# Retention, routing and expert in one kernel: one state copy, a first block cut by chunks, and rank comparisons on scores spread in PSUM

## The chip, the cores and the metric

The kernel runs on one core of one Trainium2 chip. The metric is the device time of one launch in microseconds (us). Names of engines: PE is TensorE (matrix products; PEld is its weight load), DVE is VectorE, ACT is ScalarE, POOL is GpSimd, SP is SyncE, which here only issues DMAs.

## The reference, cut to what matters

```python
# q, k, v: (batch 4, heads 8, tokens 768, 64)
gamma = 1 - 2 ** (-5 - arange(H))
for t in range(S):                                  # decayed state, one 64x64 matrix a head
    state = gamma * state + einsum('bhd,bhe->bhde', k[:, :, t], v[:, :, t])
    y[:, :, t] = scale * einsum('bhd,bhde->bhe', q[:, :, t], state)
x = y.transpose(0, 2, 1, 3).reshape(B, S, H * D)    # (4, 768, 512)
scores = einsum('bsd,d->bs', x, w_gate)
out = x.copy()
for b in range(B):                                  # 128 tokens of highest score a batch
    top = argpartition(-scores[b], 128)[:128]
    h = maximum(x[b, top] @ w1, 0)                  # 512 -> 1024
    out[b, top] = x[b, top] + sigmoid(scores[b, top])[:, None] * (h @ w2)
```

## The kernel before, in words

The recurrence is computed by chunks of 128 tokens. Twelve *blocks* of 256 tokens (i = 0 to 11, three a batch) hold two chunks each (c = 0, 1). For a block, q, k and v arrive as float32 tiles `qf`, `kf`, `vf` (512 KB each, in 2 KB packets; one partition holds eight tokens of one pair of heads). POOL scales q and v by the powers of gamma (`qc`, `vc`, line 387), ACT or POOL casts k (`kc`), all to bfloat16 "row" tiles. PE turns them (`tk`, `tq`, `tv`, line 404), ACT copies the turned tiles out of PSUM (`ek`, `eq`, `ev`, line 407), and for k and v PE turns them back into token order (`tkb`, `tvb`, line 418; copies `ekb`, `evb`, line 421).

For each chunk PE forms the scores of q against k in eight products on 64 rows of the array (`sc`, line 464, tile `ps`), DVE multiplies them with the causal mask (`mk`, line 468, tile `A`), and PE adds the part from the state and the part within the chunk (`y`, lines 475 and 478, tile `py`). The state of a batch accumulates in one PSUM tile `pst` of 4 x 128 columns: four 128x128 products a chunk (`up`, line 442) hold two heads each, and only the two 64x64 blocks on the diagonal are wanted. So two copies of 64 partitions a chunk (`es`, line 175, 64x256) move the wanted blocks to a bfloat16 tile `S`, whose other blocks POOL sets to zero at the start (`cz`, line 260). ACT copies `py` out (`ey`, tile `xo`), DVE multiplies it with the gate weights and sums (`ga`, line 501), and SP stores `xo` (`st`, line 506).

Routing needs the rank of each token's score within its batch of six chunks. For chunk J, PE spreads its 128 scores over all partitions (`pr`, line 523, a float32 transposition), ACT or DVE copies them to a float32 tile `row` (`cp`), and DVE compares: `cd` (line 530) the chunk with itself under a triangular mask `tri`, `co` (line 537) with the J earlier chunks out of `row`, one instruction of J x 128 elements. `cnt`, `rk`, `oh`, `ix`, `ic` make the list of chosen tokens. Then the expert: rows are gathered by an indirect DMA (`gat`; batch 3 picks them by a product instead), turned (`tn`), multiplied with w1 and w2 (`hu`, `dn`), scaled (`ad`) and scattered back (`sa`). The weights arrive in eight loads of 512 KB and are cast by ACT and POOL (`wc`).

The order of the work is a table, `ORDER`: each item is a task, `@A`, `@D` or `@P` name the engine where a task may run on several, and `+n` puts n filler products on PE ahead of it (line 243, operand `fill`). Each engine works through its own tasks in that order. `DEPTH` gives the number of buffers of each tile. PSUM tiles of scores, turned tiles and spread scores share one pool of five buffers, `px`.

The first block is loaded in halves by the parity of the head (two 256 KB transfers a tensor, 2 KB packets), and a tile is turned only once both halves are there.

Of the kernel before, what the change touches and what calls it, by code (L numbers as in the profile page):

```python
# [15 lines left out]

PICKED = (3,)
# [3 lines left out]
HALVES = (0,)  # L21

GATE_POOL = ()
DEPTH = {'qf': 5, 'kf': 5, 'vf': 5, 'qb': 4, 'kb': 4, 'vb': 4, 'qT': 3, 'kT': 3, 'A': 8, 'S': 6, 'xo': 15, 'junk': 2, 'sc': 3, 'row': 2, 'g': 2, 'racc': 3, 'oh': 2, 'idx': 4, 'xg': 3, 'xgT': 2, 'e': 4, 'gt': 4, 'hT': 2, 'xr': 2, 'yb': 6, 'px': 5, 'py': 2, 'pst': 1}

ORDER = """
cf lk.0.1 cd0 cp1 cd1 lv.0.1 lv.0.0 ca3 lk.0.0 kc.0.1@A cz lq.0.0 lw cp2 kc.0.0@A tk.0+13 lq.0.1 vc.0.1 lq.1.0 ca2
lk.1.0 lv.1.0 vc.0.0 lq.2.0 cp3 tv.0 cd3 lk.2.0 qc.0.0 lv.2.0 ek.0 lk.3.0 ev.0 ws wb@D tvb.0 lq.3.0 tkb.0 ekb.0 qc.0.1
qc.1.1 tq.0+2 evb.0 qc.1.0 up.0.0 eq.0 kc.1.1@A es.0.0.0@D vc.1.1 es.0.0.1@D vc.1.0 qc.2.1 sc.0.0+1 mk.0.0.0 sc.0.1
qc.2.0 kc.1.0@A vc.2.1 vc.2.0 up.0.1 tq.1 kc.3.0@P kc.3.1@P lv.3.0 lq.4.0 tk.1 lk.5.0 mk.0.0.1 y.0.0 lk.4.0 mk.0.1.0  # L30
eq.1 ek.1 tkb.1+1 ekb.1 mk.0.1.1 qc.3.0 ga.0.0 es.0.1.1@A sc.1.1 tv.1 mk.1.1.0 sc.1.0 mk.1.1.1 mk.1.0.0 kc.2.1@A y.0.1
tq.2+1 qc.3.1 ev.1 kc.2.0@A tk.2 eq.2 vc.3.0 vc.3.1 ek.2 mk.1.0.1 tvb.1 evb.1 sc.2.0+2 tv.2 es.0.1.0@D ey.0.1@D qc.4.1
lq.5.0 lv.5.0 ey.0.0@A sc.2.1 ga.0.1 up.1.0 mk.2.0.0 ev.2 qc.4.0 lv.4.0 mk.2.0.1 lq.6.0 y.1.0 mk.2.1.0 pr.0.0 lk.6.0
es.1.0.1@A tk.3 es.1.0.0@A tvb.2 y.1.1 ga.1.0 kc.4.0@P cp.0.0@D mk.2.1.1 tq.3 ek.3 evb.2 tkb.2 lq.7.0 ey.1.0@A lk.9.0
eq.3 cd.0.0 lk.7.0 ekb.2 pr.0.1 up.1.1 kc.4.1@P ga.1.1 cd.0.1 pr.0.2 sc.3.0+1 es.1.1.0@A qc.5.0 kc.5.1@P cp.0.1@A tv.3
co.0.1 es.1.1.1@A qc.5.1 ev.3 y.2.0+1 up.2.0 cp.0.2@D mk.3.0.0 mk.3.0.1 cd.0.2 sc.3.1 co.0.2 kc.5.0@A mk.3.1.0
# [93 lines left out]
def kernel(ctx: ExitStack, tc: tile.TileContext, q, k, v, w_gate, w1, w2, capacity, out):  # L130
# [52 lines left out]
    def load(i, nm):  # L183
        b, r = divmod(i, R)
        src = {"q": q, "k": k, "v": v}[nm]
        base = src[b, :, r * W:(r + 1) * W, :]
        parts = 2 if i in HALVES else 1
        tasks = []
        t = P.buf(nm + "f", [128, 1024], FT)
        for part in range(parts):  # L190
            n = 2 // parts
            ap = bass.AP(tensor=base.tensor, offset=base.offset + part * n * S * D,
                         ap=[[8 * D, W // 8], [2 * S * D, HP], [S * D, n], [1, 8 * D]])

            def issue(e, part=part, n=n, ap=ap):
                nc.sync.dma_start(t[:].rearrange("p (n x) -> p n x", n=2)[:, part * n:(part + 1) * n], ap)  # L196

            tasks.append(P.add(f"l{nm}.{i}.{part}", "SP", issue, bufs=[t]))
        loaded[nm, i] = (t, tasks)
# [13 lines left out]
    gv = consts.tile([128, R, 2, 8], FT, name="gv")  # L213
    lgm = consts.tile([128, 2], FT, name="lgm")
    causal = consts.tile([128, C], BF, name="causal")
    tri = consts.tile([128, C], BF, name="tri")
# [501 lines left out]
```

## Time and profile before

| | |
|---|---|
| Median of 3 runs | 106.24 us (106.13 to 106.3) |
| The profiled execution | 106.56 us, its span (first to last instruction) 104.7 us |
| Busy in the span | PE 91.5 us (87%), DVE 80.3 (77%), POOL 77.4 (74%), ACT 76.6 (73%) |
| DMA | 31.43 MB, 15091 packets, mean 300 GB/s |
| Mean granted TensorE clock | 0.978 |

A row of the timeline reads: start, duration, engine, source line, operation, tile written <- tiles read, number of merged instructions, and in brackets the idle time ahead of it with what ended it. A group of instructions reads: line, engine, operation, count | busy us, mean ns of one | idle us ahead of them, what ended it. The busy time of PE covers products that wait inside it, so the distance from the start of one group to the start of the next tells more than the duration.

### The profile page before, as it was taken

To read this page: it belongs to the slowest core of one execution; us is meant where nothing else is said; L and a number is where in the kernel's file an instruction comes from. 1 tells how busy PE (TensorE), PEld (TensorE's weight loads), DVE (VectorE), ACT (ScalarE), POOL (GpSimd) and SP (SyncE) were. 2 spreads that over 40 slices of the span, in tenths; PEclk is the share of its full clock that TensorE was granted. 3 is DMA by queue.
4 is the path that set the end of the run, shared out by engine and by line. 5 is a ranking of instruction groups with operands and counts; after the bars stand their busy time and mean duration, and the time that the engine had idled before them with its cause. 6 is when DMAs were issued, how large, how long until landed. Compare 5 with 4: busy or idle time off the path is not lost.

```text
span 104.7 us, 3641 instructions
## 1 busy us (share of the span) xinstructions
PE 91.5 (87%) x1416; PEld 71.6 (68%) x1416; DVE 80.3 (77%) x249; ACT 76.6 (73%) x179; POOL 77.4 (74%) x109
## 2 busy tenths in 40 slices
PE   4949879299999999899989999999899999999900
PEld 1326557168968888887878898789689985878500
DVE  5207397807999999998999999999999998254320
ACT  4444683674899999999899999999999976222200
POOL 7599669999998994979679936999893284370630
PEclk9999999967999999999999999999999999999997
DMA  1997999999999999981079999999957999972152
GB/s 22 303 299 277 336 404 390 386 386 386 391 382 386 388 387 384 388 313 41 0 271 283 343 356 401 408 418 410 386 161 228 321 399 400 388 273 108 12 88 100
DMA packets 15091, 31.43 MB, mean 300 GB/s; under 512 B 1249, under 2 KB 1249, under 8 KB 15074
## 3 DMA queue, kind: packets, MB, share of 16 engines
q1 hardware_dynamic: 14450, 29.37, 77.5%
q0 software_dynamic: 624, 1.84, 6.2%
q8 instruction: 11, 0.18, 0.7%
q14 instruction: 6, 0.05, 0.1%
HBM read 23.86 MB, written 7.34 MB: 298 GB/s over the span
## 4 chain that ended last, share of the span: by engine, by line
DMA 31%; ACT 22%; PE 14%; POOL 12%; SPq 9%; issue 8%; POOLq 1%; ACTq 0%
DMA out_dram<-xo 12%; DMA wf<-in_moe_w_dram 11%; DMA vf<-in_v_dram 8%; SPq L196 5%; ACT S L175 5%; POOL vr L387 5%; ACT xo L175 4%; SPq L506 3%; PE ps L464 2%; POOL w1s L179 2%; ACT vT L407 2%; ACT qT L407 2%; ACT kr L175 2%; ACT vb L421 2%; POOL qr L387 2%
## 5 line engine op out<-in xcount | busy, mean ns | idle before, releaser
L468 DVE TENSOR_TENSOR A<-ps,causal 128x512 bf16<-128x512 f32 x48 | 30.7, 683 | 4.1 <-PE ps L464 4.0
L387 POOL TENSOR_TENSOR qr<-qf,gq 128x512 bf16<-128x512 f32 x24 | 24.7, 1046 | 6.8 <-ACT kb L421 2.6
L387 POOL TENSOR_TENSOR vr<-vf,gv 128x512 bf16<-128x512 f32 x24 | 24.5, 1046 | 3.3 <-DMA vf<-in_v_dram 2.0
L501 DVE SCALAR_TENSOR_TENSOR junk<-py,wgB 128x512 bf16<-128x512 f32 x24 | 16.4, 683 | 0.5 <-PE py L478 0.4
L175 ACT ACTIVATE S<-pst 64x256 bf16<-64x256 f32 x37 | 14.0, 377 | 0.4
L537 DVE TENSOR_SCALAR_CACHE_REDUCE g<-row,sc,racc 128x128 bf16<-128x128 f32 (+4 forms) x20 | 13.1, 667 | 0.2
L175 ACT ACTIVATE xo<-py 128x512 f32<-128x512 f32 x22 | 13.0, 600 | 0.2
L404 PE MATMUL tk<-ident,kr 128*128 128x128 bf16 x96 | 7.5, 221 | 3.5 <-ACT kr L175 3.4
L464 PE MATMUL ps<-qT,kT 64*128 64x128 bf16 x192 | 10.0, 222 | 0.3 <-ACT kT L407 0.2
L175 ACT ACTIVATE kr<-kf 128x512 bf16<-128x512 f32 x10 | 6.2, 628 | 5.3 <-DMA kf<-in_k_dram 3.3
L478 PE MATMUL py<-vb,A 128*128 128x64 bf16 x192 | 9.5, 193 | 0.0
L404 PEld LDWEIGHTS <-kr 128*128 128x128 bf16 x96 | 5.8, 98 | 4.8 <-ACT kr L175 4.4
L421 ACT ACTIVATE kb<-tkb 128x512 f32<-128x512 f32 x12 | 7.2, 603 | 2.2 <-PE tkb L418 2.1
L464 PEld LDWEIGHTS <-kT 64*128 64x128 bf16 x192 | 5.8, 95 | 4.4 <-issue 1.0
L670 POOL DMA_INDIRECT out_dram<-xr,idx x4 | 4.7, 1168 | 5.4 <-DVE xr L664 3.0
L442 PE MATMUL pst<-vb,kb 128*128 128x128 bf16 x80 | 7.7, 219 | 1.0 <-ACT S L175 0.4
L179 POOL CAST kr<-kf 128x512 bf16<-128x512 f32 x14 | 8.3, 613 | 0.1
L530 DVE SCALAR_TENSOR_TENSOR g<-pr,sc,tri 128x128 bf16<-128x128 f32 x24 | 8.1, 345 | 0.3 <-ACT row L175 0.2
L407 ACT ACTIVATE vT<-tv 128x512 f32<-128x512 f32 x12 | 7.2, 599 | 1.4 <-PE tv L404 1.3
L475 PE MATMUL py<-S,qT 128*128 128x128 bf16 x80 | 7.7, 219 | 0.5 <-ACT xo L175 0.3
L655 PE MATMUL pd<-w2s,hT 128*128 128x512 bf16 x32 | 8.1, 379 | 0.0
L478 PEld LDWEIGHTS <-A 128*128 128x128 bf16 x192 | 7.9, 98 | 0.2
(112 smaller groups left out, 212.3 us busy)
## 6 DMA issues: line engine op xcount, KB each, us to landing
out_dram<-xo SPq DMA_DIRECT2D x24, 256.0 KB, 5.7
qf<-in_q_dram SPq DMA_DIRECT2D x11, 512.0 KB, 9.6
kf<-in_k_dram SPq DMA_DIRECT2D x11, 512.0 KB, 10.7
vf<-in_v_dram SPq DMA_DIRECT2D x11, 512.0 KB, 10.6
wf<-in_moe_w_dram SPq DMA_DIRECT2D x8, 512.0 KB, 7.7
kf<-in_k_dram SPq DMA_DIRECT2D x2, 256.0 KB, 3.9
vf<-in_v_dram SPq DMA_DIRECT2D x2, 256.0 KB, 3.5
qf<-in_q_dram SPq DMA_DIRECT2D x2, 256.0 KB, 3.9
```

Source lines behind the costliest of these rows:

```text
L175: nc.scalar.activation(dst, src, AF.Copy)
L179: nc.gpsimd.tensor_copy(dst, src)
L387: nc.gpsimd.tensor_mul(row[x][:, :, hf, :], half(x, hf), g[:, r, hf, :, None].to_broadcast([128, 8, D]))
L404: nc.tensor.transpose(t1[:, j].rearrange("p g h -> p (g h)"), row[x][:, j].rearrange("p e d -> p (e d)"), ident)
L407: return P.add(f"e{x}.{i}", "ACT", lambda e: nc.scalar.activation(words(T, "x t y").rearrange("p (x g j) -> p x g j", x=2, j=8), words(t1, ...
L421: return P.add(f"e{x}b.{i}", "ACT", lambda e: nc.scalar.activation(dst[:].rearrange("p j h d -> p (j h d)").bitcast(FT), t2[:].rearrange(" ...
L464: nc.tensor.matmul(ps[par][:, dd, :], kT[rr, dd // 2, ts, dd % 2], qT[rr, dd // 2, ts, dd % 2], start=True, stop=True, skip_group_check=True)
L468: mk = [P.add(f"mk.{i}.{c}.{par}", "DVE", lambda e, par=par: nc.vector.tensor_mul(A[par][:], ps[par][:], causal[:, None, :].to_broadcast([ ...
L478: nc.tensor.matmul(py[c][:, h, :], A[h % 2][:, h // 2, :], vb[:, c, h, :], start=(J == 0 and h == 0), stop=True, skip_group_check=True)
L501: bt["gate", J] = P.add(f"ga.{i}.{c}", "DVE", lambda e, c=c, J=J, junk=junk: nc.vector.scalar_tensor_tensor(junk[:], py[c][:].opt(), 1.0, ...
L530: nc.vector.scalar_tensor_tensor(bt["g"][:, lo + J, :], pr[:, :C], bt["sc"][:, J:J + 1], tri, OP.is_ge, OP.mult, accum_out=bt["racc"][:, J ...
L537: nc.vector.tensor_scalar(bt["g"][:, lo:lo + J, :].rearrange("p i t -> p (i t)"), bt["row"][:, :J * C], bt["sc"][:, J:J + 1], bt["racc"][: ...
```

## The change

Four edits, and a new table of order with new numbers of buffers.

**One copy a state.** Each head now has its own product: eight of 64x64 a chunk in place of four of 128x128, written to the 64 partitions of that head. At a batch's first chunk one product of zeros (128x512) clears the whole PSUM tile. `S` then takes one copy of 128x512. POOL no longer sets the `S` tiles to zero. For the last block of a batch only one of its two chunks of k is turned back.

**The first block by chunks.** Block 0 is loaded by chunks of 128 tokens (256 KB, 1 KB packets; four tokens of both heads of a pair lie in one partition), and each chunk is scaled, turned and copied by itself. That needs tables of powers of its own (`pos4`, `gq4`, `gv4`: one small instruction on POOL, two on DVE, four on ACT).

**Scores spread in PSUM.** For chunk J, PE spreads the scores of all chunks 0 to J again, up to four in one PSUM tile, and DVE compares straight from PSUM: one instruction up to J = 3, two for J = 4 and 5. The tile `row` and its copies are no longer used. The number of spreads rises from 24 to 84, that of comparing instructions falls from 44 to 32.

**Buffers and fillers.** Row tiles (`qb`) 4 to 6, `kT` 3 to 4, `vf` 5 to 4, `xo` 15 to 16; weights are loaded through the buffers of q and not of v. The fillers rise from 34 to 45, of which 28 are half as wide.

```diff
-HALVES = (0,)
+SPREAD = (0, 1, 2, 3)
+CHUNKED = (0,)
...
+        if i in CHUNKED:
+            for c in range(2):
+                ap = bass.AP(tensor=base.tensor, offset=base.offset + c * C * D,
+                             ap=[[4 * D, C // 4], [2 * S * D, HP], [S * D, 2], [1, 4 * D]])
+                tasks.append(P.add(f"l{nm}.{i}.{c}", "SP", lambda e, c=c, ap=ap: nc.sync.dma_start(
+                    t[:].rearrange("p (c n x) -> p c n x", c=2, n=2)[:, c], ap), bufs=[t]))
...
             def update(e, c=c, J=J):
-                for dd in range(HP):
-                    nc.tensor.matmul(pst[b][:, dd, :], kb[:, c, 2 * dd:2 * dd + 2, :].rearrange("p h d -> p (h d)"),
-                                     vb[:, c, 2 * dd:2 * dd + 2, :].rearrange("p h d -> p (h d)"), start=(J == 0 and dd == 0),
-                                     stop=True, skip_group_check=True)
+                if J == 0:
+                    nc.tensor.matmul(pst[b][:].rearrange("p h d -> p (h d)"), zero, fill, start=True, stop=True,
+                                     skip_group_check=True)
+                for h in range(H):
+                    hh = slice(64 * (h % 2), 64 * (h % 2) + 64)
+                    nc.tensor.matmul(pst[b][hh, h // 2, hh], kb[:, c, h, :], vb[:, c, h, :], start=False, stop=True,
+                                     skip_group_check=True)
...
-            st["es", b, J + 1] = [P.add(f"es.{i}.{c}.{par}", "ACT DVE", lambda e, Sb=Sb, hh=slice(64 * par, 64 * par + 64): copy(
-                e, Sb[hh, :, hh], pst[b][hh, :, hh]), after=[t_s, k_z], bufs=[pst[b], Sb]) for par in range(2)]
+            st["es", b, J + 1] = [P.add(f"es.{i}.{c}", "ACT DVE", lambda e, Sb=Sb: copy(e, Sb[:], pst[b][:]), after=[t_s],
+                                        bufs=[pst[b], Sb])]
...
+    def rank_spread(b, J):
...
+        for first in ((4, 0) if J > 3 else (0,)):
+            n = min(4, J + 1 - first)
+            pr = P.buf("px", [128, 512], FT, "pr")
+            def spread(e, first=first, n=n, pr=pr):
+                for I in range(n):
+                    nc.tensor.transpose(pr[:, I * C:I * C + C], bt["sc"][:, first + I:first + I + 1].to_broadcast([128, C]), identf)
...
+            def compare(e, first=first, n=n, pr=pr, near=near):
+                g = bt["g"][:, lo + first:lo + first + n, :].rearrange("p i t -> p (i t)")
+                if near:
+                    nc.vector.scalar_tensor_tensor(g, pr[:, :n * C], bt["sc"][:, J:J + 1], tri4[:, 4 * C - n * C:], OP.is_ge, OP.mult,
+                                                   accum_out=bt["racc"][:, J:J + 1])
+                else:
+                    nc.vector.tensor_scalar(g, pr[:, :n * C], bt["sc"][:, J:J + 1], bt["racc"][:, J:J + 1], OP.is_ge, OP.add,
+                                            accum_out=bt["racc"][:, J:J + 1])
```

Where the table moves instructions, at three places:

SP's queue at the start, before (tile names as above; the last figures are partitions x runs x elements):

```order
L196 DMA kf<-in_k_dram 128x1x512
L196 DMA vf<-in_v_dram 128x1x512 x2
L196 DMA kf<-in_k_dram 128x1x512
L196 DMA qf<-in_q_dram 128x1x512
L325 DMA wrow<-in_moe_w_gate_dram 1x512
L196 DMA qf<-in_q_dram 128x1x512
L196 DMA qf<-in_q_dram 128x2x512
```

The same place now (line 177 loads a chunk, line 181 a whole block):

```order
L177 DMA vf<-in_v_dram 128x2x256
L177 DMA qf<-in_q_dram 128x2x256
L177 DMA kf<-in_k_dram 128x2x256
L177 DMA qf<-in_q_dram 128x2x256
L177 DMA kf<-in_k_dram 128x2x256
L177 DMA vf<-in_v_dram 128x2x256
L181 DMA vf<-in_v_dram 128x2x512
```

The first three transfers now hold all of chunk 0, where they held all of v and one parity of k; behind block 0 stands v of block 1, where q of block 1 stood.

DVE among the tasks of blocks 1 to 3, before:

```order
L177 COPY row<-pr 128x128
L468 TENSOR_TENSOR A<-ps,causal 128x512 x2
L530 SCALAR_TENSOR_TENSOR g,racc<-pr,sc,tri 128x128
L537 TENSOR_SCALAR g,racc<-row,sc,racc 128x256
L468 TENSOR_TENSOR A<-ps,causal 128x512 x2
L501 SCALAR_TENSOR_TENSOR junk,sc<-py,wgB 128x512
L530 SCALAR_TENSOR_TENSOR g,racc<-pr,sc,tri 128x128
L537 TENSOR_SCALAR g,racc<-row,sc,racc 128x384
```

And now (line 506 is the mask, 538 the gate, 606 and 609 the comparisons out of PSUM):

```order
L506 TENSOR_TENSOR A<-ps,causal 128x512 x4
L538 SCALAR_TENSOR_TENSOR junk,sc<-py,wgB 128x512
L606 SCALAR_TENSOR_TENSOR g,racc<-pr,sc,tri_163 128x256
L506 TENSOR_TENSOR A<-ps,causal 128x512 x4
L161 COPY xo<-py 128x512
L606 SCALAR_TENSOR_TENSOR g,racc<-pr,sc,tri_163 128x384
```

The pair of comparisons has become one, and the copy to `row` is gone.

PE at a spread and an update of the state, before:

```order
L418 LDWEIGHTS kT
L418 MATMUL tkb<-ident,kT 128x128
L523 MATMUL pr<-identf,sc 128x128
L442 LDWEIGHTS kb
L442 MATMUL pst<-vb,kb 128x128
```

PE now, at the second spread of batch 0 and, in the same stretch, the last rows of an update:

```order
L515 LDWEIGHTS A
L515 MATMUL py<-vb,A 128x64
L596 MATMUL pr<-identf,sc 128x128 x2
L425 LDWEIGHTS vr
L425 MATMUL tv<-ident,vr 128x128
```

```order
L481 LDWEIGHTS kb
L481 MATMUL pst<-vb,kb 64x64
L512 LDWEIGHTS qT
L512 MATMUL py<-S,qT 128x128
L512 LDWEIGHTS qT
```

Chunk 1 now has two spreads in a row where one stood, and an update works on 64x64 pieces between groups that use the whole array.

More of the change, by code (lines that the diff above doesn't have):

```diff
@@ L32 @@
[L32 to L36, printed above, removed]
@@ L186, in load @@
         base = src[b, :, r * W:(r + 1) * W, :]
-        parts = 2 if i in HALVES else 1
         tasks = []
         t = P.buf(nm + "f", [128, 1024], FT)
[L190 to L198, printed above, removed]
+        if i in CHUNKED:
[5 more added lines that the diff above has]
+        else:
+            ap = bass.AP(tensor=base.tensor, offset=base.offset, ap=[[8 * D, W // 8], [2 * S * D, HP], [S * D, 2], [1, 8 * D]])
+            tasks.append(P.add(f"l{nm}.{i}.0", "SP", lambda e, ap=ap: nc.sync.dma_start(
+                t[:].rearrange("p (n x) -> p n x", n=2), ap), bufs=[t]))
         loaded[nm, i] = (t, tasks)
@@ L213 @@
     gv = consts.tile([128, R, 2, 8], FT, name="gv")
+    NK = len(CHUNKED)
+    assert list(CHUNKED) == list(range(NK)) and NK <= R
+    pos4_i = consts.tile([128, NK, 2, 4], I32, name="pos4_i")
+    pos4 = consts.tile([128, NK, 2, 4], FT, name="pos4")
+    gq4 = consts.tile([128, NK, 2, 2, 4], FT, name="gq4")
+    gv4 = consts.tile([128, NK, 2, 2, 4], FT, name="gv4")
     lgm = consts.tile([128, 2], FT, name="lgm")
     causal = consts.tile([128, C], BF, name="causal")
-    tri = consts.tile([128, C], BF, name="tri")
+    tri4 = consts.tile([128, (4 if SPREAD else 1) * C], BF, name="tri4")
+    tri = tri4[:, -C:]
     slot_i = consts.tile([128, C], I32, name="slot_i")
@@ L299, in c_act0, with c_act4, c_act5 @@
         nc.scalar.activation(pair, pair_i.bitcast(FT), AF.Copy)
+    def c_act4(e):
+        for par in range(2):
+            nc.scalar.activation(gq4[:, :, :, par, :], pos4, AF.Exp, bias=lnsc[:, 0:1], scale=lgp[:, par:par + 1])
+    def c_act5(e):
+        for par in range(2):
+            nc.scalar.activation(gv4[:, :, :, par, :], pos4, AF.Exp, scale=lgm[:, par:par + 1])
     def c_act2(e):
@@ L398, in turn @@
         def turn(x, cast, T):
-            t1 = P.buf("px", [128, 8, W // 8, HP], BF, "t" + x)
-            def go(e):
-                for j in range(8):
-                    nc.tensor.transpose(t1[:, j].rearrange("p g h -> p (g h)"), row[x][:, j].rearrange("p e d -> p (e d)"), ident)
-            t_1 = P.add(f"t{x}.{i}", "PE", go, after=cast + [k_p1], bufs=[row[x], t1, T], warm=warm(t1))
-            return P.add(f"e{x}.{i}", "ACT", lambda e: nc.scalar.activation(
-                words(T, "x t y").rearrange("p (x g j) -> p x g j", x=2, j=8),
-                words(t1, "j g h").rearrange("p (j g x) -> p x g j", j=8, x=2), AF.Copy), after=[t_1], bufs=[t1, T])
@@ new lines, in turn, with piece, go @@
+            if chunked:
+                return [piece(f"{i}.{c}", range(4 * c, 4 * c + 4), [cast[c]]) for c in range(2)]
+            return [piece(f"{i}", range(8), cast)] * 2
+        def back(x, e_1, T, dst):
+            def piece(name, cs, after):
+                t2 = P.buf("px", [128, len(cs), HP, 128], BF, "t" + x + "b")
+                def go(e):
+                    for k, c in enumerate(cs):
+                        for dd in range(HP):
+                            nc.tensor.transpose(t2[:, k, dd, :], T[:, dd // 2, C * c:C * c + C, dd % 2], ident)
+                t_2 = P.add(f"t{x}b.{name}", "PE", go, after=after, bufs=[T, t2, dst], warm=warm(t2))
+                return P.add(f"e{x}b.{name}", "ACT", lambda e: nc.scalar.activation(
+                    words(dst, "j h d")[:, 256 * cs[0]:256 * (cs[-1] + 1)], words(t2, "j h d"), AF.Copy), after=[t_2], bufs=[t2, dst])
+            cs = range(1 if x == "k" and r == R - 1 else 2)
+            if chunked:
+                done = [piece(f"{i}.{c}", [c], [e_1[c]]) for c in cs]
+            else:
+                done = [piece(f"{i}", cs, [e_1[0]])] * 2
+            return done
@@ L472, in y @@
             def y(e):
[L473 to L476 removed]
+                for dd in range(HP if J else 0):
+                    nc.tensor.matmul(py[c][:, 2 * dd:2 * dd + 2, :].rearrange("p h d -> p (h d)"), qT[:, dd // 2, ts, dd % 2],
+                                     S_of[b, J][:, dd, :], start=(dd == 0), stop=True, skip_group_check=True)
                 for h in range(H):
```

186 lines of the change are left out of this document (105 added, 81 removed).

## Prediction

> **What bounds the kernel now.** I read first the busy time by stretches of 12 us, because the shares of the whole span mix a start, a long middle and a tail. Columns: stretch, length, then busy us and count of PE, PEld, DVE, ACT and POOL, granted clock, DMA share, GB/s.
>
> ```profile
> 12.00:24.00 12.00, 9.12 (x127) 6.19 (x124) 7.95 (x16) 7.33 (x14) 10.68 (x12) 0.90 1.05 392
> 24.00:36.00 12.00, 11.87 (x206) 9.99 (x205) 11.44 (x33) 10.25 (x23) 11.41 (x14) 0.96 1.05 387
> 36.00:48.00 12.00, 11.63 (x204) 9.83 (x202) 11.60 (x29) 11.72 (x27) 9.88 (x12) 1.00 0.95 349
> 48.00:60.00 12.00, 11.38 (x206) 9.67 (x203) 11.74 (x41) 11.49 (x30) 10.42 (x12) 1.00 0.59 191
> 60.00:72.00 12.00, 12.00 (x234) 10.51 (x232) 11.93 (x38) 11.61 (x28) 9.39 (x12) 1.00 1.04 396
> 72.00:84.00 12.00, 11.42 (x203) 9.97 (x201) 11.96 (x38) 11.88 (x33) 7.74 (x13) 1.00 0.86 292
> 84.00:96.00 12.00, 11.95 (x161) 8.57 (x158) 7.07 (x27) 5.54 (x15) 6.26 (x9) 1.00 0.89 335
> ```
>
> From 24 to 84 us DVE works 58.7 of 60 us: it is the pace there, with ACT close behind. PE is nearly as full, but its busy time hides waiting. Its weight loads (PEld) show how full: 10.5 us in the densest stretch, 60 to 72, and a mean of 9.9 in the other four from 24 to 84. So the middle leaves PE about 6% of room, fillers included. DMA has slack (191 GB/s in one stretch). Before 24 us nothing is full. The waits of DVE say what is late there (engine, line <- releaser: us, times, longest):
>
> ```profile
> DVE A L468 <- PE ps L464: 4.0, 2, 3.5
> DVE S L177 <- PE pst L442: 1.9, 1, 1.9
> ```
>
> The start, from the timeline (POOL feeds PE, PE feeds DVE):
>
> ```profile
> GB/s 22 303 299 277 336 404 390 386 386 386 391 382 386 388 387 384 388 313 41 0 271 283 343 356 401 408 418 410 386 161 228 321 399 400 388 273 108 12 88 100
> ...
> 11.47 2.04 POOL L387 TENSOR_TENSOR qr<-qf,gq 128x512 bf16<-128x512 f32 x2 [0.92 <-DMA qf<-in_q_dram]
> 12.24 0.63 PE L464 MATMUL ps<-qT,kT 64*128 64x128 bf16 x16
> 14.50 2.04 POOL L387 TENSOR_TENSOR vr<-vf,gv 128x512 bf16<-128x512 f32 x2 [0.98 <-DMA vf<-in_v_dram]
> 19.31 0.63 ACT L175 ACTIVATE kr<-kf 128x512 bf16<-128x512 f32 x1 [2.00 <-PE tq L404]
> 20.73 1.17 POOL L179 CAST kr<-kf 128x512 bf16<-128x512 f32 x2
> 23.49 0.61 PE L464 MATMUL ps<-qT,kT 64*128 64x128 bf16 x8
> 27.51 0.61 PE L404 MATMUL tq<-ident,qr 128*128 128x128 bf16 x8
> 97.59 1.89 PE L655 MATMUL pd<-w2s,hT 128*128 128x512 bf16 x8
> ```
>
> The page's row of 40 slices (2.62 us each) shows 300 GB/s at first. The first scores of all come at 12.24, those of block 2 at 23.49, q of block 3 is turned at 27.51. The cast of k of block 2 waits 2.0 us for PE to free a row tile. The last row is the last product of the expert, ending at 99.5; 5.2 us of scaling, scattering and closing follow.
>
> PE's true costs stand in the distances between starts:
>
> ```profile
> 52.05 0.38 PE L523 MATMUL pr<-identf,sc 128*128 128x128 f32 x2
> 52.28 0.61 PE L404 MATMUL tk<-ident,kr 128*128 128x128 bf16 x8
> ...
> 54.59 0.38 PE L442 MATMUL pst<-vb,kb 128*128 128x128 bf16 x4
> 54.81 0.61 PE L418 MATMUL tkb<-ident,kT 128*128 128x128 bf16 x8
> 55.25 0.28 PE L523 MATMUL pr<-identf,sc 128*128 128x128 f32 x1
> 55.46 0.41 PE L464 MATMUL ps<-qT,kT 64*128 64x128 bf16 x8
> 55.80 0.40 PE L475 MATMUL py<-S,qT 128*128 128x128 bf16 x4
> 56.03 0.40 PE L478 MATMUL py<-vb,A 128*128 128x64 bf16 x8
> 56.27 0.61 PE L404 MATMUL tv<-ident,vr 128*128 128x128 bf16 x8
> 56.71 0.38 PE L243 MATMUL tq<-fill 128*128 128x512 bf16 x1
> 56.93 0.61 PE L404 MATMUL tq<-ident,qr 128*128 128x128 bf16 x8
> ```
>
> Two spreads take 0.23 us, so 0.11 each; four products of an update 0.22 (0.055 each); eight turns 0.44; a filler of 512 columns 0.22; eight products of 64 columns 0.24 (0.03 each). Scores use half-height pieces of the array, two side by side: eight of 128 columns would take 0.22 in pairs, yet 0.34 pass before the next group, and the single spread ahead takes 0.21 where 0.11 is its price. So entering and leaving the divided array costs about 0.1 us each.
>
> **The change part by part.** *Comparisons, DVE.*
>
> ```profile
> L530 DVE SCALAR_TENSOR_TENSOR g<-pr,sc,tri 128x128 bf16<-128x128 f32 x24 | 8.1, 345 | 0.3 <-ACT row L175 0.2
> L501 DVE SCALAR_TENSOR_TENSOR junk<-py,wgB 128x512 bf16<-128x512 f32 x24 | 16.4, 683 | 0.5 <-PE py L478 0.4
> L537 DVE TENSOR_SCALAR_CACHE_REDUCE g<-row,sc,racc 128x128 bf16<-128x128 f32 x4 | 1.6, 402 | 0.0
> L537 DVE TENSOR_SCALAR_CACHE_REDUCE g<-row,sc,racc 128x640 bf16<-128x640 f32 x4 | 3.7, 931 | 0.0
> 13.02 2.48 DVE L468 TENSOR_TENSOR A<-ps,causal 128x512 bf16<-128x512 f32 x4
> ```
>
> Removed a batch: six of 0.345 and five between 0.402 and 0.931 (mean 0.667): 5.4 us. Added, on lines through these rows: 0.345, 0.46, 0.57, 0.68 for J = 0 to 3, then 0.80 + 0.345 and 0.80 + 0.46: 4.5 us. That is 0.95 less a batch, 3.8 in all. Four masks of 0.68 take 2.48 together, so each instruction hides about 0.07 under the next, and the twelve that vanish took 0.8 less than their durations: 3.0 us saved. Bounds: 0 if comparing out of PSUM is as slow as all the old work, 4.5 if nothing was hidden. Other moves of tasks on and off DVE cancel within 0.6.
>
> *ACT and POOL.*
>
> ```profile
> L175 ACT ACTIVATE S<-pst 64x256 bf16<-64x256 f32 x37 | 14.0, 377 | 0.4
> L175 ACT ACTIVATE row<-pr 128x128 f32<-128x128 f32 x18 | 5.1, 284 | 0.0
> L175 ACT ACTIVATE xo<-py 128x512 f32<-128x512 f32 x22 | 13.0, 600 | 0.2
> L260 POOL MEMSET S<- 128x256 f32 x6 | 1.6, 322 | 0.0
> ```
>
> ACT loses 14.0 of state copies for 19 of about 0.6 (11.4), and 5.1 of row copies; it gains four small tables (about 1), some narrower pieces of block 0 (about 1) and five casts of 0.6 that POOL gives up (3). Net about 3 us less; POOL about 4 less. Neither sets the pace afterwards, so I count nothing. What waits for a state copy, the next update and the next `y`, waits for one of 0.6 and not two of 0.38 in a row.
>
> *PE.* Sixty more spreads of 0.11: +6.6 us. Four products of zeros at a filler's 0.22: +0.9. Sixteen turns of k left out at 0.055: -0.9. The update: eight products of 64 columns by pairs, like the scores (0.11), plus 0.1 in and 0.1 out, is 0.30 against 0.22. No row shows an array divided by columns. From below: 0.11, if nothing drains; from above: the spread's 0.11 per 128 columns, halved, eight times in a row, with in and out: 0.64. I take 0.30, since the scores are the nearest in kind. Twenty updates: +1.6, from -2.2 to +8.4. PE in all: +8.2 us.
>
> [...]
>
> *Start.* Chunk 0 needs three transfers of 256 KB in place of six: three less at 0.9 us (262 KB at 300 GB/s) and pieces half as long on POOL (1.0 for 2.04) bring the first scores 3.6 us earlier, to 8.6. But block 1 is no earlier: its last tensor (now q) again ends the third megabyte, which arrived by 14.5. Packets of 1 KB: bounds are half a 2 KB packet's time (no loss) and the same time (block 0's 1.5 MB, about 4 us at 392 GB/s, twice as long). I take 0.5, near the first, since the bytes are the same. From 15.0 POOL does two q (2.04), a k (0.58), two q and two v (4.1): 21.7 for v of block 2. Its turn and the scores then follow at 22.2, against 23.49, and with six row tiles the wait of 2.0 for PE is gone. PE's list up to the turn of q of block 3 is another 3.0 us of work there: 25.2, against 27.51, so 2.3 earlier. Bounds: 0 (slow packets) and 4.
>
> *Sum, on PE, from the turn of q of block 3 to the last expert product.* Before: 99.5 - 27.5 = 72.0 us. Counting the products behind that point by the prices above (a group of scores 0.44 with its gaps): 63.4 of work and fourteen fillers, 3.0. The remaining 5.6 is waiting. After, the same count gives 68.8 with updates as if undivided, plus 16 x 0.07 for entering and leaving: 69.9. Seven fillers are left: 1.5. Waiting: counted alike, the groups of the densest stretch leave 0.35 of 12 us unfilled, which is 2.1 of 72; I take that, as PE is now the fullest engine. Together 73.5, which is 1.5 longer, and it begins 2.3 earlier: -0.8 us. DVE, 3.0 lighter and 2 earlier, would allow -5; it no longer decides. The tail keeps its 5.2 us. The profiled execution took 106.56, 1.86 beyond its span and 0.3 above the median; on the median, 106.24 - 0.8 = 105.4.
>
> **Rivals.** *PE keeps up, DVE's saving comes through.* If updates cost 0.11 (16 x 0.19 = 3.0 less) and the fillers left fall into waits (0.5 less), the gain is 4.3, with DVE's limit of 5 near: 102.0. For it: DVE waits for PE in only one place after 24.2, 0.4 us for `y` by the row of L501. Against: PEld is at 10.5 of 12 already where PE is densest.
>
> *PE becomes the wall: slower.* The divided update is the mechanism: twenty groups, each between groups on the whole array. At 0.36 a group the gain is gone (0.8 / 16 = 0.05 more); at 0.45, +2.4 on the forecast, 107.8; at 0.64, 110.8. DVE would then show idle time ended by PE. For it: the rest of the added work (68.8 - 63.4 = 5.4) already takes all but 0.2 of the waiting. Against: pairs side by side work well in the scores.
>
> *Nothing measurable.* Block 0 arrives no earlier (1 KB packets 2 us slower) while PE absorbs its work, or the update is at 0.36: 106.2.
>
> **How the numbers follow.** The forecast 0.42 (104.4 to 106.0), the faster rival 0.16, the slower one 0.30, nothing 0.12. 0.2% (0.21 us) is about what a measurement of this kernel tells from no change. Faster: nearly all of the first two, less what the forecast's own range leaves within 0.2%: 0.55. Same: 0.13. Slower 0.32. The range reaches to 102.4, leaving out the better half of the faster rival, and to 108.2, leaving out updates above about 0.47.
>
> **What will show it.** Right: spreads at 0.11 in runs of up to four; an update of about 0.30 from start to start; PEld above 10.3 in each 12 us of the middle; DVE idle 2 to 5 us there, ended by PE; first scores near 8.6 us, those of block 2 near 22. Wrong: DVE still at 11.9 of 12 and a time near 102; or updates at half a microsecond; or packets of 1 KB that hold the first chunk beyond 10 us.

## The result

The changed kernel is slower by 1.3%: its runs against those of the kernel before give a ratio of 1.013 (95% interval 1.010 to 1.017). The medians of all 13 runs of each are 106.88 and 106.13 us. A second set of runs of both gave 1.018 (1.010 to 1.027). The forecast was 105.4 and faster. The profiled execution took 107.1 us with a span of 105.3.

Some executions of either kernel, of the kernel before above all, are slower (that kernel by 0.7 to 2.7% in the medians of a set), most of them at a lower granted clock (its medians 0.972 to 0.979, against 0.986 to 0.994); the times below are medians of the others, and where they and a ratio differ, most of all in experiments 2, 3, 8 and 10, the ratio rests on other runs of the kernel before, slower ones among them, and the medians count. The changed kernel stands at 106.9 us, and at 107.2 in its second set; the kernel before stands at 104.8 to 105.9, by the set.

Busy time by stretches of 12 us, columns as in the prediction (stretch, length, PE, PEld, DVE, ACT, POOL, granted clock, DMA share, GB/s):

```profile
12.00:24.00 12.00, 11.95 (x192) 8.96 (x189) 8.20 (x20) 9.61 (x22) 11.18 (x13) 1.00 1.05 388
24.00:36.00 12.00, 11.80 (x207) 9.71 (x207) 11.44 (x27) 9.88 (x20) 10.81 (x13) 1.00 1.05 383
36.00:48.00 12.00, 11.82 (x206) 10.44 (x207) 11.26 (x30) 9.81 (x21) 12.00 (x14) 1.00 0.89 320
48.00:60.00 12.00, 11.75 (x255) 10.68 (x254) 11.73 (x29) 10.43 (x21) 8.77 (x12) 1.00 0.92 311
60.00:72.00 12.00, 12.00 (x219) 10.43 (x218) 10.84 (x33) 10.00 (x20) 10.85 (x12) 1.00 0.99 366
72.00:84.00 12.00, 11.18 (x208) 9.99 (x208) 10.79 (x31) 10.43 (x23) 5.40 (x11) 1.00 1.00 367
84.00:96.00 12.00, 11.89 (x175) 9.62 (x174) 7.17 (x24) 5.61 (x14) 3.63 (x5) 1.00 0.55 198
```

DVE has come down from 58.7 to 56.1 of the 60 us from 24 to 84, and PE is full (11.2 to 12.0 of 12 us) from 12 us on, not from 24. What DVE waits for, by group (line, releaser last):

```profile
L538 DVE SCALAR_TENSOR_TENSOR junk<-py,wgB 128x512 bf16<-128x512 f32 x24 | 16.2, 685 | 2.7 <-PE py L515 2.3
L606 DVE SCALAR_TENSOR_TENSOR g<-pr,sc,tri 128x128 bf16<-128x128 f32 (+3 forms) x24 | 11.8, 502 | 3.2 <-PE pr L596 3.0
L609 DVE TENSOR_SCALAR_CACHE_REDUCE g<-pr,sc,racc 128x512 bf16<-128x512 f32 x8 | 6.4, 811 | 1.5 <-PE pr L596 1.0
```

The comparisons take 18.2 us against 8.1 + 13.1 = 21.2, the 3.0 that the prediction counted; and they now wait 4.0 us for spreads on PE. In the chain of work that ended last, PE now holds the most (it was DMA 31%, ACT 22%, PE 14%):

```profile
PE 60%; DMA 12%; issue 10%; DVE 5%; POOL 4%; SPq 3%; POOLq 1%; ACT 1%; DVEq 0%; ACTq 0%
```

PE, from the timeline:

```profile
8.67 0.40 PE L502 MATMUL ps<-qT,kT 64*128 64x128 bf16 x8 [0.20 <-ACT kT L429]
...
17.05 0.81 PE L236 MATMUL tq<-fill 128*128 128x512 bf16 x2
17.70 0.61 PE L425 MATMUL tq<-ident,qr 128*128 128x128 bf16 x8
...
19.80 0.50 PE L236 MATMUL tkb<-fill 128*128 128x256 bf16 x3
...
22.85 0.41 PE L502 MATMUL ps<-qT,kT 64*128 64x128 bf16 x8
...
26.03 0.61 PE L425 MATMUL tq<-ident,qr 128*128 128x128 bf16 x8
...
55.27 0.62 PE L445 MATMUL tkb<-ident,kT 128*128 128x128 bf16 x8
55.83 0.32 PE L481 MATMUL pst<-vb,kb 128*64 128x64 bf16 x8
56.07 0.18 PE L633 MATMUL pk<-later,pair 128*128 128x6 bf16 x1
...
98.69 0.55 PEld L730 LDWEIGHTS <-hT 128*128 128x128 bf16 x4
```

First scores at 8.67, those of block 2 at 22.85, q of block 3 turned at 26.03. The last four expert products begin at 98.7 and end, by the 1.03 us that four of the same shape take at 97.75, at 99.7. Between the turns of the start stand fillers (line 236). An update takes 0.24 from its start to the start of the next group, and the turn ahead of it 0.56 where 0.44 is its price.

### The profile page after: what moved, and what is told of

The parts are those of the page before. It is cut to its first block, busy times and chain, and to the rows that moved or that the text cites. A ratio compares the mean times of both kernels' runs of the same rounds, so it can differ in the third digit from the quotient of the medians.

```text
span 105.3 us, 3854 instructions
## 1 busy us (share of the span) xinstructions
PE 93.4 (89%) x1547; PEld 77.2 (73%) x1555; DVE 78.9 (75%) x226; ACT 73.5 (70%) x155; POOL 74.1 (70%) x103
## 4 chain that ended last, share of the span: by engine, by line
PE 60%; DMA 12%; issue 10%; DVE 5%; POOL 4%; SPq 3%; POOLq 1%; ACT 1%; DVEq 0%; ACTq 0%
PE pr L596 8%; DMA xg<-out_dram,idx 7%; PE ps L502 6%; DMA vf<-in_v_dram 5%; PE tq L425 5%; PE tvb L445 5%; PE tv L425 5%; PE py L515 5%; PE py L512 4%; PE tk L425 4%; PE pst L481 4%; PE tkb L445 4%; PE ph L716 3%; SPq L177 3%; POOL out_dram L745 3%
## 5 line engine op out<-in xcount | busy, mean ns | idle before, releaser
L606 DVE SCALAR_TENSOR_TENSOR g<-pr,sc,tri 128x128 bf16<-128x128 f32 (+3 forms) x24 | 11.8, 502 | 3.2 <-PE pr L596 3.0
L596 PE MATMUL pr<-identf,sc 128*128 128x128 f32 x84 | 13.9, 278 | 0.0
L159 ACT ACTIVATE S<-pst 128x512 bf16<-128x512 f32 x19 | 11.4, 602 | 0.4 <-PE pst L481 0.4
L425 PE MATMUL tv<-ident,vr 128*128 128x128 bf16 x96 | 7.5, 220 | 2.1 <-POOL vr L404 2.1
L596 PEld LDWEIGHTS pr<-identf,sc 128*128 128x128 f32 x84 | 8.9, 137 | 0.4
L429 ACT ACTIVATE qT<-tq 128x512 f32<-128x512 f32 (+1 forms) x13 | 7.4, 572 | 2.5 <-PE tq L425 2.5
L448 ACT ACTIVATE vb<-tvb 128x512 f32<-128x512 f32 (+1 forms) x13 | 7.4, 569 | 2.3 <-PE tvb L445 2.0
L716 PE MATMUL ph<-xgT,w1s 128*128 128x128 bf16 x128 | 8.5, 219 | 0.0
L716 PEld LDWEIGHTS <-w1s 128*128 128x128 bf16 x128 | 7.7, 98 | 0.8
L429 ACT ACTIVATE kT<-tk 128x512 f32<-128x512 f32 (+1 forms) x13 | 7.4, 567 | 1.1 <-PE tk L425 1.1
```

The source lines that it names most:

```text
L159: nc.scalar.activation(dst, src, AF.Copy)
L425: nc.tensor.transpose(t1[:, k].rearrange("p g h -> p (g h)"), row[x][:, j].rearrange("p e d -> p (e d)"), ident)
L429: return P.add(f"e{x}.{name}", "ACT", lambda e: nc.scalar.activation(words(T, "x t y").rearrange("p (x t) -> p x t", x=2)[:, :, lo:lo + 32 ...
L596: nc.tensor.transpose(pr[:, I * C:I * C + C], bt["sc"][:, first + I:first + I + 1].to_broadcast([128, C]), identf)
L606: nc.vector.scalar_tensor_tensor(g, pr[:, :n * C], bt["sc"][:, J:J + 1], tri4[:, 4 * C - n * C:], OP.is_ge, OP.mult, accum_out=bt["racc"][ ...
L716: nc.tensor.matmul(ph[:, j, :], w1s[:, dd, lo:lo + 255:2], xgT[:, dd, :], start=(j == 0 and dd == 0), stop=True, skip_group_check=True)
```

## Experiments

Each is a change of one part, or of the order of the work. "After" is the changed kernel, "before" the other. The runs were made in five sets, each with before beside it: before stood at 105.2 us in the set of experiments 1, 4 and 5; at 105.5 in that of 2, the second runs of after, the first run of 6 and the first of 8; at 105.9 in that of 3, the second run of 6, before without fillers in 8 and the first run of 10; at 104.8 in that of 7, the repeat in 8 and the second run of 10; and at 105.3 in that of 9 and the last run of 8.

**1. PE's work doubled where it was added.** After, with

```diff
-                for I in range(n):
+                for I in [x for x in range(n) for _ in range(1 if first + x == J else 2)]:
                     nc.tensor.transpose(pr[:, I * C:I * C + C], ...)
```

> The changed kernel, with each of the 60 added spreads made twice: 6.6 us more on PE, nothing else. Theory 1, PE became the pace: every microsecond counts, 112.5 to 113.5. Theory 2, PE still has room and the loss lies elsewhere: part of it fits into waits, below 109.

112.9 us (ratio 1.076, 1.072 to 1.080): 6.0 us more for 6.6 of work. Busy time by stretches:

```profile
36.00:48.00 12.00, 11.82 (x213) 10.29 (x208) 10.44 (x27) 9.31 (x19) 11.89 (x13) 1.00 0.79 270
60.00:72.00 12.00, 12.00 (x231) 10.58 (x230) 10.42 (x29) 9.59 (x19) 10.50 (x13) 1.00 0.90 323
```

DVE drops to 10.4 of 12 while PE stays full. So PE is the pace of the changed kernel when work is added to it.

**2. The same spreads in before, with nothing saved.** Into each spread of chunk J:

```diff
+            for I in range(J):
+                nc.tensor.transpose(pr[:, C + I % 3 * C:2 * C + I % 3 * C], bt["sc"][:, J:J + 1].to_broadcast([128, C]), identf)
```

> The kernel before, with 60 idle spreads more on PE, as many as the change adds, into columns that nothing reads: 6.6 us of PE's work, nothing on other engines. The prediction's sum lets waiting fall from 5.6 to 2.1 us, so that 3.5 of it are absorbed: 2.5 to 4 us slower than before. If PE was full before already: 6 to 6.6 slower. If DVE's pace hides it: less than 1.

109.7 us against 105.5: 4.2 us for 6.6 of work. The ratio, 1.031 (1.023 to 1.039), would make it 3.3. So before had room for a third to a half of that work; the prediction's waiting term (5.6 falls to 2.1) has it take up 3.5, about half.

**3. Spread comparisons alone, in before and its order.**

```diff
-    pr.b.J -> cp.b.J (ACT) ; cd.b.J, co.b.J (DVE)      rank_part as it was
+    pr.b.J, pr.b.J.0 -> cs.b.J, cs.b.J.0               rank_spread in its place
```

> The kernel before with spread comparisons alone: 60 spreads more on PE (6.6 us, as in the run with idle spreads, which cost 2.95), DVE 3 us less, ACT 5 less. If what DVE and ACT save counts as in the prediction, about 1 us more than before, 107 to 108.5, as PE takes part of it back. If PE alone decides: 109.5 to 110.5, as with idle spreads. If DVE was the pace in the middle and PE had room: 1 to 2 us faster than before.

109.6 us against 105.9, so 3.7 us slower (ratio 1.027, 1.017 to 1.037): within half a microsecond of the run with idle spreads. DVE's 3 us and ACT's 5 bought at most that much in this order. PE is nearly full in this run (11.8 to 12.0 of 12 us in each stretch from 24 to 72) and DVE is not (10.6 to 11.4).

**4. The old comparisons in the new order.**

```diff
-SPREAD = (0, 1, 2, 3)
+SPREAD = ()          # cp on ACT behind each pr, cd and co where cs stood; row buffers paid with one less of xo, S and A
```

> The changed kernel, with the rank comparisons as they were (one spread a chunk, ACT's copies of rows, DVE's two steps), the rest of the change and its table of order kept. PE has 60 spreads of 0.11 us less, 6.6 us; DVE gets 3 us back and ACT 5. Theory 1, PE became the pace: 1.5 to 2.5 us below the changed kernel, 104.4 to 105.4, where DVE stops it again, busy 11.6 of 12 in the middle. Theory 2, the loss lies in the new order, at the start and in the tail, and DVE's saving was real: 2 to 3 us above the changed kernel, 109 to 110.

112.1 (ratio 1.068, 1.056 to 1.080): worse than either theory. The groups show why:

```profile
L161 ACT ACTIVATE row<-pr 128x128 f32<-128x128 f32 x20 | 5.3, 282 | 7.6 <-PE pr L562 7.6
L569 DVE SCALAR_TENSOR_TENSOR g<-pr,sc,tri 128x128 bf16<-128x128 f32 x24 | 8.2, 348 | 4.5 <-ACT row L161 4.3
```

ACT waits 7.6 us for PE ahead of the copies, whose places I put in by hand, and DVE waits 4.3 us for ACT. This says nothing on PE: it prices a table that no longer fits its tasks.

**5. One copy of the state, undone in after and done alone in before.**

```diff
-  nc.tensor.matmul(pst[b], zero, fill) ; 8 x matmul(pst[hh, h // 2, hh], kb[:, c, h], vb[:, c, h]) ; copy(S, pst)
+  4 x matmul(pst[:, dd], kb[:, c, 2 * dd:2 * dd + 2], vb[...]) ; 2 x copy(S[hh, :, hh], pst[hh, :, hh])
```

> The changed kernel, with the state kept in two copies as it was: four products of 128x128 an update and no products of zeros, two copies of 64 rows on ACT. PE has 20 x 0.12 + 0.9 = 3.3 us less, ACT 2.6 more. Theory 1, PE became the pace: 2 to 3 us below the changed kernel, 104 to 105. Theory 2: no faster than the changed kernel, 106.7 to 108, since the two copies in a row hold the next update.

> The kernel before, with one copy of the state alone: products of zeros and updates by heads on PE (+3.3 us), one copy an update on ACT (2.6 less). Theory 1, PE had only a few us of room: 1 to 2.5 us slower than before. Theory 2, ACT's copies were holding DVE: 0.5 to 1 us faster. If PE had room enough and ACT's copies held nothing: the same within 0.3.

Undone in after: 1.013 (0.997 to 1.029), with only three runs to go by, 106.0, 106.6 and 107.5: unclear. Alone in before: 105.6 against 105.2, a ratio of 1.006 (0.999 to 1.012): at most 1.2% slower. What this run did show is the start. Stretches, columns as above, first before, then before with one copy, then block 2's scores and the turn of q of block 3 in the timeline of the latter:

```profile
18.00:21.00 3.00, 0.96 (x14) 0.48 (x10) 2.66 (x6) 1.67 (x4) 2.86 (x4) 1.00 1.04 382
21.00:25.00 4.00, 3.87 (x35) 2.65 (x36) 0.86 (x2) 2.25 (x5) 3.80 (x5) 0.57 1.05 387
```

```profile
18.00:21.00 3.00, 0.96 (x12) 0.63 (x12) 2.17 (x5) 1.86 (x4) 2.94 (x4) 1.00 1.05 386
21.00:25.00 4.00, 3.85 (x74) 3.21 (x73) 2.31 (x4) 2.96 (x6) 3.87 (x6) 1.00 1.05 387
```

```profile
22.25 0.40 PE L448 MATMUL ps<-qT,kT 64*128 64x128 bf16 x8
...
25.68 0.61 PE L384 MATMUL tq<-ident,qr 128*128 128x128 bf16 x8
```

Both leave PE idle for 2 of the 3 us from 18 to 21. In the profiled execution of before the granted clock then fell to a mean of 0.57 over the next 4 us, and PE did 35 products there; in the other it did not fall, PE did 74, and block 3's q is turned at 25.68, not 27.51. The half rate lasted from 21.5 to 24.9, 3.4 us (0.50 to 0.57 by the clock column in each half microsecond), and came behind an idle gap of 1.9 us on PE. Behind one of 1.8 us in the other run it did not come, nor behind one of 1.9 us in before without 21 fillers (experiment 8); what decides it is not shown.

**6. Fewer spreads in after, comparisons kept.** Batches 0 to 2 compare out of shared tiles:

```diff
-            pr = P.buf("px", [128, 512], FT, "pr")              # a tile of spreads for each chunk
+            pr = lent.setdefault((b, lead, first), ...)         # chunks 0 to 3 one tile; 4 and 5 two
```

> The changed kernel, with the spread scores of batches 0 to 2 used more than once: one tile of four spreads serves the comparisons of chunks 0 to 3, one more tile of four and one of two those of chunks 4 and 5. All comparisons stay as they are; PE makes 33 spreads less, 3.6 us. Theory 1, PE is the pace: 3 to 3.6 us below the changed kernel, 103.3 to 104. Theory 2, the loss lies in the order, the start and the tail: 106.4 to 107.5. A third way: tiles of scores are held longer and DVE gets its comparisons late, so that part of it is lost again: 104.5 to 106.

107.2 us (ratio 1.013, 1.007 to 1.018), where after itself stood at 107.2 in the same set: no gain from 3.6 us. The comparisons had to move together behind the shared tile; DVE is at 11.7 to 11.8 of 12 us from 36 to 60, and PE fell to 10.7 in the second stretch:

```profile
36.00:48.00 12.00, 11.69 (x220) 10.22 (x218) 11.73 (x35) 9.59 (x20) 12.00 (x14) 1.00 0.93 320
48.00:60.00 12.00, 10.72 (x220) 9.29 (x219) 11.82 (x31) 9.70 (x20) 10.89 (x14) 1.00 0.98 333
```

So I took PE's work away without moving anything:

```diff
-                for I in range(n):
+                nc.tensor.matmul(pr[:, :(n - 1) * C], fill[:, :128], fill[:, :(n - 1) * C], ...)   # if n > 1
+                for I in [n - 1]:
                     nc.tensor.transpose(pr[:, I * C:I * C + C], ...)
```

> The changed kernel, order and waits kept; of each group of spreads only the last is made, and one bf16 product of ones fills the other columns, so that ranks are not computed and the first 128 tokens of each batch are routed. 52 spreads of 0.11 us become 52 x 128 columns at 0.055: 2.9 us less on PE, spread over 18 to 88 us. Theory 1, PE is the pace from end to end: 2.2 to 2.9 us below the changed kernel, 104.2 to 104.9. Theory 3, the start held by fillers decides, and in the middle other waits take over what PE gives up: less than 1 us, 106.2 to 107.2.

105.8 us (ratio 1.000, 0.993 to 1.007): 1.1 to 1.4 us below after for 2.9 us of work, between the theories. Its profiled execution, 108.2 us long, waits 2.6 us on PE for gathered tokens:

```profile
PE pg L695 <- DMA xg<-out_dram,idx: 2.6, 2, 1.6
```

**7. Are the gathers the next limit?** The turns of the gathered tokens moved behind the attention, in after and in the kernel of the run above:

```diff
- ... mk.11.0.0 tn.0 mk.11.0.1 pr.3.2 tn.1 ... up.11.0 cnt.2 y.11.0 ... es.11.0@A y.11.1
+ ... mk.11.0.0 mk.11.0.1 pr.3.2 ... up.11.0 cnt.2 y.11.0 ey.10.1@A ga.10.1 tn.0 ... es.11.0@A ... y.11.1 tn.1
```

> The changed kernel, with the turns of the gathered tokens of batches 0 and 1 moved behind the two y of block 11 on PE (the state copy and y of its second chunk come ahead of them). In the changed kernel PE waits 1.0 us for that gather at 77 us. Theory 4, the landing of the gathers is a second limit right behind PE: 0.4 to 1 us below the changed kernel, 106 to 106.5. Rival, the masks of block 11 take its place: the same within 0.4.

> The kernel with 2.9 us less of spreads on PE (ranks not computed, the first 128 tokens of each batch routed), and the same move of the two turns. There PE came to the gathers earlier and waited 2.8 us for them. Theory 4: what PE gave up now shows, 104 to 105.2. Rival, DVE (11.8 of 12 us busy from 24 to 72 us in that run) or the masks take it: 106 to 107.

107.5 us (ratio 1.027, 1.021 to 1.033) and 105.2 (1.002, 0.993 to 1.010). In after the move loses 0.3 to 0.6, by the set of after it is held against; PE, which waited 0.8 us for the gather there, now waits 1.0 for DVE's multiplication with the gate weights to give up its `py`:

```profile
PE py L513 <- DVE junk L539: 1.0, 1, 1.0
```

With lighter spreads it gains 0.6, inside the spread of the runs. So the theory of the gathers is not shown. What stands out in the trace of that last run is DVE:

```profile
24.00:36.00 12.00, 11.80 (x211) 9.54 (x210) 11.78 (x27) 10.08 (x20) 11.17 (x13) 1.00 1.05 385
36.00:48.00 12.00, 11.83 (x231) 10.36 (x223) 11.77 (x33) 10.29 (x21) 12.00 (x14) 1.00 0.92 324
60.00:72.00 12.00, 12.00 (x235) 10.37 (x235) 11.80 (x35) 10.53 (x21) 9.16 (x11) 1.00 1.00 359
```

With 2.9 us less on PE, DVE is back at 11.8 of 12 from 24 to 72 us. That makes DVE the likely second limit, about 1 to 1.5 us behind PE; no run took work off both, so it is not shown.

**8. Fillers.** All but those of the first two groups left out (`tv.1+2` becomes `tv.1`, and so on): 27 in after, twice run, 21 in before; then only after's 20 ahead of block 3's turn of q.

> The changed kernel, with the 27 filler products behind the first two groups left out, 3.9 us of PE's work, some 2.4 of it before 27 us. Theory 1 in its strict form, PE is full from 12 us on and the fillers cost what they take: 1.5 to 3.9 us below the changed kernel, 103 to 105.4. Rival: they lie in waits: the same within 0.5, or up to 1.5 us slower if the granted clock falls in the gaps that open.

> The changed kernel without the 27 fillers once more, beside the other three: 105.3 to 105.8 by every theory.

> The kernel before, with its 21 filler products behind the first turn left out, 4.6 us of PE's work. Theory 3, fillers cost time only where PE has no waiting, which in the kernel before is nowhere in the start (PE 9.1 of 12 us there) and little in the middle: within 0.7 of before. Rival, fillers cost what they cost in the changed kernel, half of their length: 1.5 to 2.3 us faster than before. The other way: the granted clock falls in the gaps, up to 1.5 slower.

> The changed kernel, with only the 20 fillers ahead of the turn of q of block 3 left out (behind the first two groups); the seven behind it stay. Theory 3, the fillers of the start are what held it: all of the gain of the run without any, 105.2 to 106. Rival, the seven later ones cost their 1.5 us too: 106.2 to 107.

After without 27: 105.5 us, 1.7 below after in the same set, and 105.6 when repeated. Only the first 20 left out: 105.5, all of the gain. Before without 21: 105.8 against 105.9, a ratio of 1.006 (0.998 to 1.015), nothing. By their widths the 20 fillers are 3.3 us of work (ten of 0.11 and ten of 0.22, as in the trace of after three of 256 columns take 0.34 from 19.80 to the next start, and one of 512 takes 0.22 from 19.04), where the expectations count 2.4; the seven behind them are 1.5. In the trace of after without 27, block 3's turn of q, and the last expert products:

```profile
23.81 0.61 PE L425 MATMUL tq<-ident,qr 128*128 128x128 bf16 x8
...
96.65 0.55 PEld L730 LDWEIGHTS <-hT 128*128 128x128 bf16 x4
```

2.2 us earlier than in after at the first, 2.0 at the last. The fillers that the new table puts into the start held everything behind it; the seven later ones lay in waits. The same turn, and the last expert products, in the trace of before without 21, where the granted clock stayed at 1.00 from 18 to 28 us:

```profile
25.23 0.61 PE L404 MATMUL tq<-ident,qr 128*128 128x128 bf16 x8
...
96.45 1.89 PE L655 MATMUL pd<-w2s,hT 128*128 128x512 bf16 x8
```

Held against before in the same set, after without 27 stands at 105.5 us against 105.5 (ratio 0.988, 0.981 to 0.995), its repeat at 105.6 against 104.8 (1.007, 1.002 to 1.011), and after without the first 20 at 105.5 against 105.3 (1.002, 0.998 to 1.007). So leaving the fillers out wins back what the change had lost; it is not shown to beat the kernel before.

**9. The chunked start undone**, in after without fillers: block 0 loaded and turned whole.

```diff
-CHUNKED = (0,)
+CHUNKED = ()          # tasks of the two chunks of block 0 joined in the table; 9 fillers of 512 columns ahead
```

> The changed kernel without the 27 fillers, and with block 0 loaded and turned whole, in 2 KB packets, items of its two chunks joined in the table. First scores near 12 us in place of 9. If the chunked start carries on to the end, as the prediction had it (2.3 us at the turn of q of block 3): 1.5 to 2.5 us above the kernel without fillers, 107 to 108. Rival, what comes early is lost again at the loads, which run at 385 to 390 GB/s from 12 to 36 us either way: within 0.7, 105 to 106.3.

107.8 us (ratio 1.026, 1.020 to 1.032), 2.3 us above the kernel without fillers. First scores and turn of q of block 3:

```profile
12.70 0.40 PE L505 MATMUL ps<-qT,kT 64*128 64x128 bf16 x8
...
27.64 0.61 PE L428 MATMUL tq<-ident,qr 128*128 128x128 bf16 x8
```

Against this version the chunks bring the first scores from 12.7 to 9.4 us (without fillers), and 2.3 of those 3.3 us reach the end. But the 2.3 is not the chunks' alone: this table, joined by hand, turns q of block 3 at 27.64, where before without 21 fillers, its block 0 whole as well, does so at 25.23 (experiment 8). Held against that start, after without fillers is 1.4 us earlier at this turn (23.81). The loads do not take it all back.

**10. A version to beat both**: after without 27 fillers, and seven groups of spreads (17 spreads) taken from tiles that are still there; then with the move of 7.

```diff
+LENT = {'0.5.0': '0.3', '1.4.0': '1.5.0', '2.5.0': '2.4.0', '2.1': '2.2', '2.0': '2.2', '2.4': '2.5', '3.0': '3.1'}
```

> The changed kernel without the 27 fillers (105.5 in its own run), and seven groups of spreads left out where a tile with the same columns is still there (17 spreads, 1.9 us of PE), comparisons almost in the old places. Theory 1: 103.5 to 104.2. Theory 3: 104.9 to 105.7, no gain beside the fillers, since the waits of 24 to 84 us take it up.

> The changed kernel without the 27 fillers, without 17 spreads that stand in a tile already, and with the same move of the two turns. Theory 4: 103.6 to 104.8. Rival: 105.2 to 105.8, as without the move.

105.4 us against 105.9 of before (ratio 0.989, 0.982 to 0.995) and 105.8 against 104.8 (1.012, 1.000 to 1.024): no better than without fillers alone, and not shown to beat the kernel before.

## Why the prediction was wrong

*The step that failed is the start.* The prediction gave it 2.3 us, from 27.51 to 25.2 at the turn of q of block 3. Both ends were wrong. The first came from an execution with PE at half rate from 21.5 to 24.9; the quoted row of 12 to 24 us had 0.90 in its clock column, and I did not read it. Where the clock held, the start of before reaches that turn at 25.68 (with one copy of the state) and at 25.23 (without 21 fillers). The second end left out the fillers: I counted them behind that turn and not the 20 ahead of it, and it came at 26.03. Leaving them out brings it to 23.81, so 25.2 was not too bold for the work itself. Against a start at full clock (25.68) the changed kernel begins 0.35 late. What the new start brings was also put too high: without fillers on either side it is 1.4 us at that turn and not 2.3 (experiment 9), and the fillers, 2.2 us there, take more than that.

The prediction also read that before 24 us nothing is full. Its own row of 12 to 24 us has the DMA engines at a share of 1.05 and 392 GB/s. They did not hold the 2.2 us back: without the fillers that stretch still moves 389 GB/s.

*PE's sum held.* Forecast 73.5 us from that turn to the end of the last expert product, measured 99.7 - 26.0 = 73.7. Spreads cost 0.11 as priced (eight in 0.88, from 53.06 to 53.94, and 6.0 for 60 in experiment 1). An update costs 0.24, and up to 0.12 more for the turn ahead of it: 0.36 and not 0.30, some 1 us over 16. As the sum came out all the same, another term, presumably the waiting, was smaller by about as much; that is luck. The update's 0.36 lies between the prediction's bounds of 0.11 and 0.64; what makes up the 0.12 is not shown. That before had room on PE for part of the added work was right: a third to a half, by experiment 2.

*The tail* grew from 5.2 to 5.6, which I held fixed. Summed on the profiled spans: 1.5 earlier, 1.7 longer and 0.4 at the end make +0.6, from 104.7 to 105.3. Against a before whose clock holds the loss is larger. The start of experiment 5 put to the rest of the profiled run gives 25.7 + 72.0 + 5.2 = 102.9, an estimate, and a loss of 2.4. That is too much, since an early start is in part lost again: before without 21 fillers is at that turn at 25.2 and takes 73.1 us from there to the end of the last expert product. With 73.1 the estimate is 104.0 and the loss 1.3, inside the 1.0 to 1.8 us that the interval of the ratio gives.

*The rivals.* The slower one had the right side and a wrong mechanism: dear updates. What made the kernel slower was 5.4 us of plain work that the waiting in before covers only in part, with no head start to pay for the rest. "PE keeps up" is refuted by experiment 1. That DVE "would allow -5" looks too generous: experiment 7 finds DVE at 11.8 of 12 again after 1 to 1.5 us.

*The signs listed* came true in the main: spreads at 0.11, DVE idle 3.9 us from 24 to 84 and ended by PE, first scores at 8.67 and those of block 2 at 22.85. PEld was above 10.3 in three of the five stretches, where each had been named, and an update took 0.24 from start to start, not 0.30. None of them tested the sign of the result. What stays open: what the one copy of the state is worth, what the chunks alone are worth, and what holds the kernel at 105.4 without fillers.

## What to carry to other kernels

Before a start or a stretch is used as the base of a difference, read its clock column: here an idle gap of 1.9 us on PE was followed by 3.4 us at half rate in one profiled execution and by none in another. Fillers are work where their engine is full (leaving out 27 gained 1.7 us in the changed kernel, leaving out 21 nothing in before); count them along the whole path, from time zero. Work taken from the pacing engine and put on the next fullest can pay only up to the distance between the two, so weigh both sums before moving anything.

## What the runs showed of the hardware

An idle gap of 1.8 to 1.9 us on PE, ending between 20.2 and 21.2 us, was followed by 3.4 us at half rate in two profiled executions (before, from 21.5 to 24.9, mean granted clock 0.57 from 21 to 25; before with idle spreads, from 20.2 to 23.6, mean clock 0.86 from 12 to 24) and by none in two others (before with one copy of the state, before without 21 fillers, both at 1.00 from 18 to 25).

Pieces of 64 columns of the array load their weights eight times in 0.20 us:

```profile
55.82 0.20 PEld L481 LDWEIGHTS <-kb 128*64 128x64 bf16 x8
```

No cost of the 1 KB packets shows in the first 12 us. For each unit of time that the DMA engines are busy, the changed kernel without fillers moves 248 GB/s at a share of 0.76, which is 326, and the changed kernel, with the same loads, 244 at 0.80, which is 305. With 2 KB packets it is 234 at 0.71, which is 330, in before, and 293 at 0.81, which is 362, in experiment 9. Kernels with packets of one size differ by as much as the two sizes do, and the loads are issued in different orders. The prediction's 0.5 us for the packets is isolated by no run. The rows, in this order:

```profile
0.00:12.00 12.00, 8.59 (x82) 6.18 (x83) 5.20 (x32) 6.92 (x19) 9.12 (x30) 1.00 0.76 248
0.00:12.00 12.00, 7.53 (x81) 5.29 (x83) 4.77 (x32) 6.97 (x19) 8.79 (x29) 1.00 0.80 244
0.00:12.00 12.00, 8.70 (x62) 4.59 (x62) 4.17 (x27) 6.10 (x12) 9.02 (x30) 1.00 0.71 234
0.00:12.00 12.00, 5.90 (x27) 3.07 (x28) 3.32 (x29) 5.09 (x12) 9.10 (x26) 1.00 0.81 293
```
